# Window attention over a 511 x 511 image: one hand-ordered pipeline of blocks in place of a scheduled one

## The chip, the cores and the metric

The kernel runs on one core of a Trainium2 chip. The metric is the device time of one execution in microseconds (us). A core has a matrix engine (PE, with its weight loads in a row of their own, PEld), a vector engine (DVE), a scalar engine (ACT), GpSimd (POOL), and a sync engine (SP) that here only issues transfers. Sixteen DMA engines move data between the chip's memory (HBM) and the on-chip SBUF. PE writes to PSUM, from where DVE and ACT bring results to SBUF (an "eviction").

## The reference

```python
# x: 1 x 511 x 511 x 192, bf16; ws = 7, nh = 4 heads, dh = 48
pe = sum over the 3x3 taps of (x shifted) * dw_pe      # depthwise, zero padding
x0 = x + pe
h = layernorm(x0)                                      # over the 192 channels
hw = h cut into 73 x 73 windows of 7 x 7 = 49 tokens
q, k, v = split(hw @ w_qkv)
attn = softmax(einsum('whnm', q, k) * dh ** -0.5)
out = einsum('wnhd', attn, v) @ w_o
return x0 + out (windows put back)
```

There are 5329 windows of 49 tokens.

## The kernel before, in words

**Blocks.** 128 windows lie on the 128 partitions and make a block; 42 blocks cover the image in row order, the last with 81 windows. `XC` (two buffers) holds a block's pixels, 49 tokens x 192 channels in each partition; the convolution is added into it, and at the end the attention's output, and it is stored from there. `XP` (one buffer) holds the 9 x 9 patch around each window, transposed: patch position on 81 partitions, windows and channels along them.

**Convolution** (`conv_tile`, L274). For each channel one matmul of K = 81: the weights loaded are the patches `XP[0:81, :, c]` of 128 windows, every 192nd element of a partition, and the moving operand is a table `T` of 49 columns built once at the start. Twenty channels fill a PSUM buffer of two banks, and one DVE instruction (L284) adds them into `XC`.

**Layer norm.** `stats_part` (L301) gives DVE one `bn_stats` for each token, `stats_fin` a chain of small DVE instructions for 1/std. `build_D` (L324) lets POOL multiply the identity by 1/std, and `transposes` (L336) uses that diagonal as moving operand: seven matmuls bring seven tokens transposed and scaled into PSUM, and ACT or DVE (L355, L357) copies them to `hT`.

**Attention** runs over 16 groups of 8 windows in a block. `stage_A` (L402): q and k, 8 matmuls of 392 columns (L412) and their evictions (q in two halves into `Qb`, which is block-diagonal over pairs of heads, L421 and L422; k at L424 or L426), then v with 8 matmuls of 192 columns (L431, eviction L438). `stage_B` (L443): 16 matmuls of scores (L453) with all 128 rows and half of the array's columns each, and one exponential on ACT (L478). `stage_D` (L525): 32 matmuls (L532) on two 64 x 64 tiles of the array, a reciprocal and a multiplication on DVE (L543, L544). `stage_E` (L553): 8 matmuls against the identity turn the result (L560), and ACT copies it to `OT` (L567). `proj` (L359) multiplies `OT` by `w_o` when a block is done, with `XC` added by a matmul against the identity (L377) in one half of the buffers and by DVE (L378) in the other.

**What sets the order.** The main loop (L587) writes the stages down for group after group; a scheduler of the language may shift them within an engine. The convolution of the next block is written into groups 7 to 10 (`CONV0`, three `conv_tile` each), the statistics into groups 11 to 15, the transposes at a block's first group, `proj` and the store at group 3. All PSUM work goes through one ring of four two-bank buffers, `ps`. Loads of `XC` are on POOL's queue (L108); loads of `XP` (L139), in DMAs of nine patch rows by up to 73 windows with one 384-byte piece for each patch position and window, and the stores (L396) are on SP's queue.

Of the kernel before, what the change touches and what calls it, by code (L numbers as in the profile page):

```python
# [32 lines left out]
@with_exitstack  # L33
def _window_attn_kernel(ctx: ExitStack, tc: tile.TileContext, x, dw_pe, w_qkv, w_o, out, fast=None, eps=1e-5, logit_lim=40.0):
    nc = tc.nc
    _, H, W, C = x.shape
    WS, NH = 7, 4
    DH = C // NH
    S = WS * WS
    NWR, NWC = H // WS, W // WS  # L40
    NWIN = NWR * NWC
    BLK = 128
    NBLK = (NWIN + BLK - 1) // BLK
    KP = 81
    KT = C // 2
    CH = 8
    NCH = BLK // CH
    TOK = CH * S
    scale = float(DH) ** -0.5
    assert C == 192  # L50

    xr = x[0].rearrange("h (b q) c -> h b q c", q=WS)
    outr = out[0].rearrange("(a r) (b q) c -> a b r (q c)", r=WS, q=WS)
    xw = x[0].rearrange("(a r) (b q) c -> a b r (q c)", r=WS, q=WS)

    consts = ctx.enter_context(tc.tile_pool(name="consts", bufs=1))
    big = ctx.enter_context(tc.tile_pool(name="big", bufs=1))
    psum = ctx.enter_context(tc.tile_pool(name="psum", bufs=1, space=bass.MemoryType.PSUM))

    PS = _Rot([psum.tile([128, 1024], F32, name=f"ps{i}") for i in range(4)])  # L60
    for i, t in enumerate(PS.t):
        nc.vector.memset(t[:], 0.0)

    def two_bank(ps, ncol):
        return ps[:].rearrange("p (b n) -> p b n", b=2)[:, :, 0:ncol]

    ident = consts.tile([128, 128], BF, name="ident")
    make_identity(nc, ident[:])
    ones = consts.tile([128, 128], BF, name="ones")
    nc.vector.memset(ones[:], 1.0)  # L70

    XP = big.tile([128, BLK, C], BF, name="XP")
    XPf = XP[:].rearrange("p n c -> p (n c)")
    XC = [big.tile([128, S, C], BF, name=f"XC{i}") for i in range(2)]

    wq_sb = [consts.tile([128, 3 * C], BF, name=f"wq_sb{kt}") for kt in range(2)]
    Wo = [consts.tile([128, C], BF, name=f"Wo{kt}") for kt in range(2)]
    dwK = consts.tile([32, C], BF, name="dwK")
    nc.vector.memset(dwK[:], 0.0)
    for j in range(3):  # L80
        nc.sync.dma_start(out=dwK[9 * j : 9 * j + 3, :], in_=dw_pe[:, j, :])
    for kt in range(2):
        nc.scalar.dma_start(out=wq_sb[kt][0:KT, :], in_=w_qkv[kt * KT : (kt + 1) * KT, :])
        nc.scalar.dma_start(out=Wo[kt][0:KT, :], in_=w_o[kt * KT : (kt + 1) * KT, :])

    T = big.tile([128, C, S], BF, name="T")
    Sel = XC[1][:].rearrange("p n c -> p (n c)")[0:32, 0 : S * KP]
    nc.vector.memset(XP[:], 0.0)
    nc.vector.memset(XC[0][:], 0.0)

    def segments(blk):
        n0 = blk * BLK
        n1 = min(n0 + BLK, NWIN)
        segs = []
        n = n0
        while n < n1:
            a, b0 = divmod(n, NWC)
            b1 = min(NWC, b0 + (n1 - n))
            segs.append((a, b0, b1, n - n0))
            n += b1 - b0  # L100
        return segs

    def load_xc(blk):
        xc = XC[blk % 2]
        for (a, b0, b1, p0) in segments(blk):
            for o in range(0, b1 - b0, 16):
                nb = min(16, b1 - b0 - o)
                nc.gpsimd.dma_start(  # L108
                    out=xc[p0 + o : p0 + o + nb].rearrange("p (r q) c -> p r (q c)", q=WS), in_=xw[a, b0 + o : b0 + o + nb]
                )  # L110

    def load_xp(blk):
        for (a, b0, b1, p0) in segments(blk):
            nb = b1 - b0
            if a == NWR - 1 and blk > 0:
                nc.gpsimd.memset(XP[0:KP, p0 : p0 + nb, :], 0.0)
            else:
                if b0 == 0:
                    nc.gpsimd.memset(XP[0:9, p0 : p0 + 1, :], 0.0)
                if b1 == NWC:  # L120
                    nc.gpsimd.memset(XP[64:KP, p0 + nb - 1 : p0 + nb, :], 0.0)
            pr0 = 1 if a == 0 else 0
            pr1 = 8 if a == NWR - 1 else 9
            h0 = WS * a - 1
            for pc in range(9):
                if pc == 0:
                    q, sh = WS - 1, -1
                elif pc == 8:
                    q, sh = 0, 1
                else:  # L130
                    q, sh = pc - 1, 0
                bb0, bb1 = b0, b1
                if pc == 0 and bb0 == 0:
                    bb0 = 1
                if pc == 8 and bb1 == NWC:
                    bb1 = NWC - 1
                if bb1 <= bb0:
                    continue
                nc.sync.dma_start(  # L139
                    out=XP[9 * pc + pr0 : 9 * pc + pr1, p0 + bb0 - b0 : p0 + bb1 - b0, :],  # L140
                    in_=xr[h0 + pr0 : h0 + pr1, bb0 + sh : bb1 + sh, q, :],
                )


    load_xc(0)
    load_xp(0)

    nc.gpsimd.memset(Sel, 1.0)
    nc.gpsimd.affine_select(
        out=Sel,  # L150
        in_=Sel,
        compare_op=ALU.is_equal,
        fill=0.0,
        base=0,
        pattern=[[-1, WS], [-9, WS], [1, KP]],
        channel_multiplier=-1,
    )
    s0 = 0
    n = 0
    while s0 < S:  # L160
        ns = min(4, S - s0)
        ps = PS.next()
        for ss in range(ns):
            col = (ss // 2) * 512 + (ss % 2) * C
            nc.tensor.matmul(
                ps[0:KP, col : col + C],
                lhsT=Sel[0:21, (s0 + ss) * KP : (s0 + ss + 1) * KP],
                rhs=dwK[0:21, :],
                start=True,
                stop=True,  # L170
            )
        for bk in range((ns + 1) // 2):
            nn = min(2, ns - 2 * bk)
            dst = T[0:KP, :, s0 + 2 * bk : s0 + 2 * bk + nn].rearrange("p c s -> p s c")
            src = ps[0:KP, bk * 512 : bk * 512 + nn * C].rearrange("p (s c) -> p s c", c=C)
            if n % 2 == 0:
                nc.vector.tensor_copy(out=dst, in_=src)
            else:
                nc.scalar.copy(out=dst, in_=src)
            n += 1  # L180
        s0 += ns

    nc.vector.memset(XC[1][:], 0.0)

    Wqk = [consts.tile([128, 4, 128], BF, name=f"Wqk{kt}") for kt in range(2)]
    Wv = [consts.tile([128, C], BF, name=f"Wv{kt}") for kt in range(2)]
    pcs = PS.next()
    for kt in range(2):
        nc.tensor.matmul(pcs[:, 0 : 2 * C], lhsT=ones[0:KT, :], rhs=wq_sb[kt][0:KT, 0 : 2 * C], start=(kt == 0), stop=(kt == 1))
    for kt in range(2):  # L190
        nc.tensor.matmul(pcs[:, 512 : 512 + C], lhsT=ones[0:KT, :], rhs=wq_sb[kt][0:KT, 2 * C : 3 * C], start=(kt == 0), stop=(kt == 1))
    for kt in range(2):
        nc.vector.memset(Wqk[kt][:], 0.0)
        nc.vector.scalar_tensor_tensor(
            out=Wqk[kt][0:KT].rearrange("p m (h e) -> p (m h) e", e=64)[:, :, 0:DH],
            in0=pcs[0:KT, 0 : 2 * C].rearrange("p (g d) -> p g d", d=DH),
            scalar=-1.0 / C,
            in1=wq_sb[kt][0:KT, 0 : 2 * C].rearrange("p (g d) -> p g d", d=DH),
            op0=ALU.mult,
            op1=ALU.add,  # L200
        )
        nc.vector.scalar_tensor_tensor(
            out=Wv[kt][0:KT, :],
            in0=pcs[0:KT, 512 : 512 + C],
            scalar=-1.0 / C,
            in1=wq_sb[kt][0:KT, 2 * C : 3 * C],
            op0=ALU.mult,
            op1=ALU.add,
        )


    if fast is None:
        onesf = consts.tile([128, 1], F32, name="onesf")
        nc.vector.memset(onesf[:], 1.0)
        wsq = consts.tile([128, 2 * C], F32, name="wsq")
        nrm = [consts.tile([128, 8], F32, name=f"nrm{kt}") for kt in range(2)]
        for kt in range(2):
            nc.vector.tensor_tensor(out=wsq[0:KT, :], in0=wq_sb[kt][0:KT, 0 : 2 * C], in1=wq_sb[kt][0:KT, 0 : 2 * C], op=ALU.mult)
            nc.vector.tensor_reduce(out=nrm[kt][0:KT, :], in_=wsq[0:KT, :].rearrange("p (g d) -> p g d", d=DH), op=ALU.add, axis=AX.X)
# [14 lines left out]
    def main(fast):  # L234
      with ExitStack() as mctx:
# [342 lines left out]
        for it in range(NCT):  # L578
            conv_tile(0, it)
# [110 lines left out]
```

## Time and profile before

| what | us |
|---|---|
| median of three runs (5340.39 to 5368.98) | 5347.22 |
| span of the profiled execution | 5337.2 |
| PE busy, in all | 4490.1 |
| DVE busy | 3816.7 |
| ACT busy | 2744.5 |
| POOL busy | 758.0 |
| start, up to the first matmul of q | 157.5 |
| last block, from its first matmul of q | 94.6 |

The profiled span lies 10 us under the median. Between the start and the last block lie 41 blocks in 5085.1 us, 124 us each. In the profile a row of a group of instructions gives its line, engine, shape, count, busy time and the mean duration of one, and then what ended the engine's idle time before it. In a table of windows each row is a stretch of time with each engine's busy time in it, the granted PE clock (1.00 is full speed) and the DMA engines' busy share.

The rows of the matmuls give their latency (a matmul of 392 columns has 380 ns). In a stream they overlap, and what counts for PE is the distance from start to start: worked out from the trace's start times, the middle one is 170 ns in L412 (392 columns), 82 ns in L431 and L369 (192 columns), 55 ns in L346 (128 columns), 45 ns in L560 (98 columns) and 88 ns in L282, the convolution.

### The profile page before, as it was taken

The numbers are of one execution on the slowest core, as the hardware profiler recorded it, in microseconds if no ns is written. First come the engines' busy times: TensorE is split into PE (matmuls) and PEld (weight loads), VectorE is DVE, ScalarE is ACT, GpSimd is POOL, SyncE is SP. The second block draws the span as 40 slices with busy tenths as digits, with TensorE's granted clock in tenths as the row PEclk, the third lists the DMA queues.
The fourth block names the chain that finished last, engine by engine and source line by source line (L and its number), as shares of the span: only waits on it lengthen the run. The fifth ranks groups of instructions, "written<-read, shape, count | busy, mean of one in ns | idle before, by whom it ended". The sixth has DMA issues, their size and how long they took to land.

```text
span 5337.2 us, 148265 instructions
## 1 busy us (share of the span) xinstructions
PE 4490.1 (84%) x65427; PEld 3661.5 (69%) x65427; DVE 3816.7 (72%) x6912; ACT 2744.5 (51%) x3385; POOL 758.0 (14%) x833
## 2 busy tenths in 40 slices
PE   2788888888888888888988888888888888888887
PEld 1666676667776676677776777767666776677776
DVE  6776777767776777777677777777777777767776
ACT  1554555545555555555555455555555555545555
POOL 1111111111111111111111111111111111111120
PEclk9887888887778887888788877788888888877888
DMA  6554445554455555554455544455555445544431
GB/s 67 51 75 70 68 71 80 82 73 68 68 68 70 71 72 74 71 74 71 68 73 91 75 68 68 68 72 72 74 72 72 73 70 78 85 74 67 68 48 32
DMA packets 512613, 375.27 MB, mean 70 GB/s; under 512 B 453129, under 2 KB 453321, under 8 KB 511958
## 3 DMA queue, kind: packets, MB, share of 16 engines
q1 hardware_dynamic: 480918, 265.08, 38.1%
q0 software_dynamic: 30592, 100.32, 10.6%
q8 instruction: 514, 8.42, 0.7%
q14 instruction: 141, 1.16, 0.1%
q10 hardware_dynamic: 448, 0.30, 0.0%
HBM read 265.31 MB, written 100.27 MB: 68 GB/s over the span
## 4 chain that ended last, share of the span: by engine, by line
PE 44%; DVE 16%; ACT 14%; DMA 12%; SPq 9%; issue 4%; POOL 1%; DVEq 0%; ACTq 0%; POOLq 0%
PE ps L412 12%; PE ps L282 8%; SPq L396 7%; DMA out_dram<-XC 7%; PE ps L369 6%; DMA XC<-in_x_dram 5%; PE ps L453 5%; PE ps L532 4%; DVE kT L424 4%; ACT hT L355 4%; DVE Qb L422 3%; PE ps L431 2%; DVE XC L284 2%; PE ps L560 2%; ACT kT L426 2%
## 5 line engine op out<-in xcount | busy, mean ns | idle before, releaser
L412 PE MATMUL ps<-hT,Wqk 96*128 96x392 bf16 x5336 | 1233.5, 380 | 76.7 <-DVE XC L284 62.2
L478 ACT ACTIVATE PT<-ps 128x784 bf16<-128x784 f32 x667 | 552.7, 829 | 1095.3 <-PE ps L453 1080.3
L421 ACT CAST Qb<-ps 64x784 bf16<-64x784 f32 x667 | 555.3, 833 | 657.5 <-PE ps L412 655.7
L412 PEld LDWEIGHTS <-Wqk 96*128 96x128 bf16 x5336 | 529.4, 108 | 486.1 <-issue 252.5
L284 DVE TENSOR_TENSOR XC<-ps,XC 128x980 bf16<-128x980 f32 x378 | 437.9, 1176 | 503.0 <-PE ps L282 247.2
L282 PE MATMUL ps<-T,XP 81*128 81x49 bf16 x8064 | 744.0, 264 | 55.5 <-DMA XP<-in_x_dram 55.5
L567 ACT CAST OT<-ps 96x784 bf16<-96x784 f32 x667 | 541.0, 811 | 456.0 <-PE ps L560 452.4
L282 PEld LDWEIGHTS <-XP 81*128 81x128 bf16 x8064 | 733.9, 220 | 57.6 <-issue 55.5
L431 PE MATMUL ps<-Wv,hT 96*128 96x192 bf16 x5336 | 663.5, 277 | 16.4 <-DVE On L544 9.0
L532 PE MATMUL ps<-V,PT 49*64 49x49 bf16 x21344 | 542.5, 195 | 159.1 <-DVE Qb L422 81.2
L431 PEld LDWEIGHTS <-hT 96*128 96x128 bf16 x5336 | 548.8, 111 | 180.0 <-issue 91.6
L544 DVE TENSOR_TENSOR On<-ps,rs 128x768 bf16<-128x768 f32 x667 | 634.6, 951 | 16.0
L532 PEld LDWEIGHTS <-PT 49*64 49x64 bf16 x21344 | 466.2, 116 | 260.4 <-issue 217.7
L327 POOL TENSOR_TENSOR D<-ident,rstd 128x896 bf16<-128x896 bf16 x294 | 486.2, 1681 | 1074.8 <-DVE rstd L320 1053.3
L424 DVE CAST kT<-ps 128x784 bf16<-128x784 f32 x462 | 450.0, 974 | 219.2 <-PE ps L412 209.1
L304 DVE BATCH_NORM_STATS2 bnst<-XC 128x6 f32<-128x192 bf16 x2058 | 600.5, 343 | 0.2
L453 PE MATMUL ps<-Qb,kT 128*64 128x98 bf16 x10672 | 408.0, 225 | 180.7 <-DVE Qb L422 132.2
L422 DVE CAST Qb<-ps 64x784 bf16<-64x784 f32 x462 | 451.6, 978 | 110.6 <-ACT Qb L421 100.1
L355 ACT CAST hT<-ps 96x896 bf16<-96x896 f32 x462 | 452.4, 1109 | 135.9 <-PE ps L346 134.9
L560 PE MATMUL ps<-ident,On 128*96 128x98 bf16 x5336 | 412.1, 226 | 114.4 <-DVE kT L424 110.9
L453 PEld LDWEIGHTS <-kT 128*64 128x64 bf16 x10672 | 341.5, 121 | 231.5 <-issue 131.7
L108 POOL DMA_DIRECT2D XC<-in_x_dram x386 | 216.0, 560 | 1865.9 <-DVE rs L543 996.3
(73 smaller groups left out, 4396.2 us busy)
## 6 DMA issues: line engine op xcount, KB each, us to landing
XC<-in_x_dram POOLq DMA_DIRECT2D x277, 294.0 KB, 7.5
out_dram<-XC SPq DMA_DIRECT2D x277, 294.0 KB
XP<-in_x_dram SPq DMA_DIRECT2D x210, 246.4 KB
XP<-in_x_dram SPq DMA_DIRECT2D x68, 243.0 KB
XC<-in_x_dram POOLq DMA_DIRECT2D x37, 165.4 KB, 7.1
out_dram<-XC SPq DMA_DIRECT2D x37, 165.4 KB
XP<-in_x_dram SPq DMA_DIRECT2D x22, 216.0 KB
XP<-in_x_dram SPq DMA_DIRECT2D x18, 212.6 KB
```

The lines of the kernel that those rows point to most:

```text
L282: nc.tensor.matmul(ps[:, col : col + S], lhsT=XP[0:KP, :, c], rhs=T[0:KP, c, :], start=True, stop=True)
L304: nc.vector.bn_stats(out=bnst[:, s, :], in_=xc[:, s, :])
L355: nc.scalar.copy(out=hv[0:KT, kt, :, s0 : s0 + NDG], in_=src)
L412: nc.tensor.matmul(ps[:, ab * 512 : ab * 512 + TOK], lhsT=Wqk[kt][0:KT, which * 2 + ab, :], rhs=hT[0:KT, kt, ck * CH : (ck + 1) * CH, 0:S] ...
L421: nc.scalar.copy(out=dst[0:64, :, :, 0, :], in_=src[0:64])
L422: (nc.vector.tensor_copy if dve_help else nc.scalar.copy)(out=dst[64:128, :, :, 1, :], in_=src[64:128])
L424: nc.vector.tensor_copy(out=dst[:, :, 0:TOK], in_=two_bank(ps, TOK))
L431: nc.tensor.matmul(ps[:, col : col + C], lhsT=hT[0:KT, kt, ck * CH + 2 * jj : ck * CH + 2 * jj + 2, :].rearrange("p w s -> p (w s)"), rhs= ...
L453: nc.tensor.matmul(ps[64 * wp : 64 * wp + 64, col : col + 2 * S], lhsT=k_[:, ab, w * S : w * S + 64], rhs=q_[:, ab, w, :, :].rearrange("p ...
L478: nc.scalar.activation(out=pt[:, 0 : 16 * S].rearrange("p (b n) -> p b n", b=2), in_=two_bank(ps, 8 * S), func=ACTF.Exp, scale=scale,)
L532: nc.tensor.matmul(ps[64 * wp : 64 * wp + 64, col : col + S], lhsT=pt[64 * wp : 64 * wp + S, pc_ : pc_ + 64], rhs=v_[64 * wp : 64 * wp + S ...
L544: nc.vector.tensor_tensor(out=o_[:].rearrange("p (b j) (h d) -> p b (j h) d", b=2, d=DH), in0=ov[:, :, :, 0:DH], in1=r_[:].rearrange("p (b ...
```

## The change

The kernel is written anew, as a class, and the order within each engine is now fixed by hand (`tc.manual_schedule()`). What it computes is the same.

- **Blocks** are made of two strips of 64 windows (`_blocks`), 42 in all, the last with 81 windows. Pixels lie in `X`, three buffers. All loads and stores of full blocks are on SP's queue, in DMAs of 64 partitions: `X` row by row (14 DMAs for a block), stores in four chunks of rows (8 DMAs). `XP` keeps one buffer but is ordered by patch row first: a DMA's nine rows now go to partitions 9 apart, and not to nine neighbours.
- **Convolution**: same matmuls, in PSUM buffers of one bank (two of them, `psc`, shared with the transposes), ten channels each. They are put between the matmuls of q, k and v by `fill`, over the first 7.5 of a block's 16 slots; where a following block allows it, its first 30 channels are done in slots 14 and 15 already.
- **Layer norm**: `bn_stats` reads two tokens, interleaved, in one instruction (25 and not 49 for a block); POOL computes 1/std with a power and multiplies the pixels by it (`ln_norm`); PE transposes in its transpose mode with bf16 in PSUM (`ln_tr`); one half of each is copied by DVE, the other by ACT. This goes over slots 9 to 15, and the result goes to `HO`, two buffers, in which `stage_E` later puts the attention's output in the place of its own input.
- **Attention**: q is one eviction, no longer block-diagonal. Scores and attention times v are 32 matmuls each, in turn on all four 64 x 64 tiles. `stage_E` uses the transpose mode. All evictions of q, k and the exponential are on ACT; those of v on DVE in slots 0 to 7 and 15, on ACT otherwise; those of `stage_E` on DVE. The other PSUM ring has three two-bank buffers.
- **Projection**: two tiles of four tokens in each of slots 2 to 6, the rest in 7 and 8; ACT copies, POOL adds into `X`. The matmuls against the identity are gone.

```diff
-    XP[9 * pc + pr0 : 9 * pc + pr1, p0 + bb0 - b0 : p0 + bb1 - b0, :]
+    self.XPr = self.XP[0:KP].rearrange("(r q) n c -> q r n c", q=9)
+    dst = XPr[pc, pr0:pr1, p0 + n0 : p0 + n1, :]
...
-            for s in range(sa, sb):
-                nc.vector.bn_stats(out=bnst[:, s, :], in_=xc[:, s, :])
+            nc.vector.bn_stats(
+                out=bnst[:, s : s + 2, :].rearrange("p a f -> p (a f)"),
+                in_=self.X[b % 3][:, s : s + 2, :].rearrange("p s c -> p c s"),
+            )
+        def ln_norm(b, r, eng):
+            t = slice(r * WS, (r + 1) * WS)
+            e = nc.gpsimd
+            e.tensor_scalar(out=rstd[:, t], in0=bnst[:, t, 2], scalar1=1.0 / C, scalar2=self.eps, op0=ALU.mult, op1=ALU.add)
+            e.tensor_tensor(out=rstd[:, t], in0=rstd[:, t], in1=expo[:].to_broadcast([128, WS]), op=ALU.pow)
...
+            eng.tensor_tensor(
+                out=h[:, :, :], in0=self.X[b % 3][:, t, :], in1=rstd[:, t].unsqueeze(2).to_broadcast([128, WS, C]), op=ALU.mult
+            )
+        def stage_A(b, ck, which, fill):
...
+            for ab in range(2):
+                for kt in range(2):
+                    mm(
+                        ps[:, ab * 512 : ab * 512 + TOK],
+                        lhsT=self.Wqk[kt][0:KT, which * 2 + ab, :],
+                        rhs=HO[b % 2][0:KT, kt, ck * CH : (ck + 1) * CH, 0:S],
...
+                fill(2)
+            nc.scalar.copy(out=dst[:, :, 0:TOK], in_=two_bank(ps, TOK))
...
+                        for hp, cp in ((0, 0), (1, 1), (0, 1), (1, 0)):
+...
+                                tile_position=(64 * hp, 64 * cp),
...
+            conv_goal = base + part(0.0, 0.39 + d, C - base)
+            ahead = n and conv.c == C and early and xpn == len(xp) and xln == len(xl)
+            if ahead:
+                conv, conv_goal = nn.conv, 10 * part(0.875, 1.0, 3)
...
+            s_goal = part(0.40 + d, 0.87, len(n.items)) if n else 0
...
+                    goal = part(0.38 + d, 0.64 + d, len(xp), at)
+                    while xpn < goal:
+                        xp[xpn]()
...
+                stage_A(b, ck, 0, fill if not ahead else lambda w: None)
+                stage_E(*groups[g - LE], nc.vector.tensor_copy)
+                stage_A(b, ck, 1, fill)
+                stage_V(b, ck, fill, nc.vector.tensor_copy if idle else nc.scalar.copy, vv[g % 2])
...
+                stage_D(vv[(g - LD) % 2])
+                stage_B()
+                    n.transpose(part(0.50 + d, 0.96, WS), 1.0)
```

In a block in the middle, the matmuls of slots 0 to 6 hold 22 channels of convolution each and slot 7 holds 8; slots 2 to 6 have 16 matmuls of the projection, slot 7 has 8 and slot 8 has 10; slots 9 to 15 have 14 transposes of the layer norm each; slots 14 and 15 have 20 and 10 channels of the block after next. On SP's queue the 18 DMAs of `XP` begin behind the convolution's last matmul in slot 7; the stores of the last two chunks stand between them, and the 14 of `X` at their end and behind. DVE's first addition of channels in slot 14 waits for all DMAs of `X`.

## The prediction

> **What bounds the kernel now.** I read the page's busy times first, then a table of windows over one block, then the timeline of an ordinary slot, and last SP's queue.
>
> ```profile
> span 5337.2 us, 148265 instructions
> PE 4490.1 (84%) x65427; PEld 3661.5 (69%) x65427; DVE 3816.7 (72%) x6912; ACT 2744.5 (51%) x3385; POOL 758.0 (14%) x833
> ```
>
> No engine is full over the span, so the limit must change by stage. The table cuts the block that begins at 2018.4 us: two ordinary slots, the slot with the projection, four ordinary ones, the convolution, and slots with statistics and transposes.
>
> ```profile
> core 0: us, PE busy (x) PEld busy (x) DVE busy (x) ACT busy (x) POOL busy (x), PEclk, DMA share, GB/s
> 2018.36:2027.96 9.60, 7.72 (x148) 5.97 (x145) 7.94 (x9) 5.84 (x8) 0.00 (x0) 1.00 0.75 79
> 2027.96:2042.36 14.40, 13.97 (x197) 12.92 (x196) 10.42 (x13) 6.82 (x10) 0.00 (x0) 1.00 0.41 44
> 2042.36:2061.40 19.04, 15.40 (x293) 11.90 (x290) 15.88 (x19) 10.40 (x14) 3.48 (x7) 1.00 0.88 190
> 2061.40:2100.40 39.00, 36.24 (x414) 30.42 (x409) 23.36 (x26) 7.56 (x10) 1.55 (x3) 0.53 0.22 33
> ```
>
> The fourth row is the expensive one: 39 us in which ACT and POOL do nearly nothing and the PE clock is granted by half. In that stretch the trace has four groups' work and 192 channels in solid runs; a channel has 88 ns from start to start, of which its 49 columns fill a quarter, and the matmuls of q and k, 170 ns apart elsewhere, are 327 ns apart. Ordinary slots take 4.8 us, in which DVE has 4.1 us of work (0.26 + 0.95 + 0.97 + 0.98 + 0.96).
>
> ```profile
> 1903.04 0.54 PE L453 MATMUL ps<-Qb,kT 128*64 128x98 bf16 x16 [0.49 <-DVE Qb L422]
> 1903.51 0.69 PE L532 MATMUL ps<-V,PT 49*64 49x49 bf16 x32
> 1904.13 1.54 PE L412 MATMUL ps<-hT,Wqk 96*128 96x392 bf16 x8
> ```
>
> From start to start: scores 0.47 us, attention times v 0.62 us. SP's queue, columns start and length:
>
> ```profile
> 1854.07 54.74 SPq L139 DMA_DIRECT2D XP<-in_x_dram  x27
> ```
>
> One block's `XP`, 128 x 81 pieces of 384 bytes (3.98 MB), keeps the queue 54.7 us. Before, that lay beside slots 11 to 15 and the next block's first, and nobody waited.
>
> **PE, slot by slot.** q and k are unchanged, 8 x 170 = 1.36 us; v 8 x 82 = 0.66. `stage_E`: 128 columns and not 98, 8 x 55 (the distance in L346) = 0.44, before 0.36. Scores and attention times v, 32 matmuls each: the 0.62 us of 32 on two tiles is the upper end, half of it (four tiles fully beside each other) the lower; I take 0.5 each, nearer the row, since more pairs must also be issued. Together 3.46. A channel costs at most 88 ns; behind a matmul of 170 or 82 ns its weights load under that one, and the lower end is some 50 ns. I take 70: 22 channels 1.54. Projection, 16 x 82 = 1.31. So slots 0 and 1 are 5.0, slots 2 to 6 are 6.3, slot 7 is 4.7, slot 8 is 4.3.
>
> In slots 9 to 13 PE has 3.46 + 14 x 55 ns = 4.2, but DVE more: reciprocal and product 1.21, `stage_E`'s copy 0.9 (0.81 on ACT, 0.96 on DVE for such shapes), a transposed half 1.16 (L357), and 25 / 6.5 of the new `bn_stats`. Its row is 343 ns for 192 elements, 292 back to back (600.5 us for 2058); 192 elements more at about a nanosecond each make 0.49: 1.86. DVE: 5.1. The bounds are 0.3 (a faster read) and 0.69 (two old ones), 0.7 us a slot either way. Slots 14 and 15: 3.46 + 0.77 + 15 x 0.07 = 5.3 on PE.
>
> Sum: 10 + 31.5 + 4.7 + 4.3 + 25.5 + 10.6 = 86.6 us. An ordinary slot before stood 0.65 us over its fullest engine, one at ACT's limit (4.53 with 4.1 of work) 0.4; I add 0.4 a slot: 93 us for a block, where it is now 124 (5085 / 41).
>
> **What is moved beside this.** ACT per block: 48 evictions of q, k and exponentials at 0.83, seven v at 0.81, seven halves at 1.11, 13 copies at 0.8, together 64 us of 93; DVE about 77: both are hidden. POOL: 13 additions of 768 elements and 7 products of 1344 at 1.88 ns each (L327: 1681 ns for 896) are 18.7 + 17.6 us; DVE's instructions have no two SBUF inputs with them. Power of 128 x 7 has no row: 0.25 us (the small memsets, L119) is the floor; I take 1, and 5 as upper end. POOL then needs 7 x (2.5 + 0.25 + 1) = 26 us within slots 8 to 15, hidden; at 5 it is 54, some 12 more than is there. Adding the pixels on POOL removes 25 x 82 ns of identity matmuls and DVE's L378. The removed chain of small DVE instructions is in the 77.
>
> **The transfers.** This is where a new wait comes. `XP` has one buffer, so its load starts behind the convolution's last matmul in the middle of slot 7, 47 us into the block. Slot 14 needs it again, and DVE's first addition there needs all of `X`, at 84 us. All is on one SP queue: behind a late DMA wait the ones of `X`, behind DVE's addition everything DVE does for attention, and then PE. So 37 us must suffice for `XP`, two chunks of stores (384 pieces of 2688 bytes) and `X` (896). Such a piece takes 135 ns in the middle on SP's queue: (384 + 896) x 0.135 / 16 = 10.8 us.
>
> By the row `XP` takes 54.7 us again, a wait of 54.7 + 10.8 - 37 = 28 us. But its rows now lie nine partitions apart. [...] Counting the trace's 384-byte pieces by the microsecond gives 190 in the middle and 323 in the fastest hundredth, when DMAs have drifted apart. I take 323: 10368 / 323 = 32 us, 32 + 10.8 - 37 = 6 us of wait. A block: 99 us.
>
> **The clock.** [...] I take nothing, since q, k and v are in every slot.
>
> **Start, end, sum.** The start has 109.7 us until `XP` has landed, with DVE's zeroing ahead of it and two blocks' `XC` beside; alone with one block's `X` I estimate 32 + 18 + 10 for setting up = 60. Then channels 17 (192 x 88), statistics 12, seven rows of norm and transposes 25: 115, before 157.5. The last block: 11 slots at 4.9 and a final projection (8 us), store and two slots' rest: 80, before 94.6. 115 + 41 x 99 + 80 = 4254 us of span, and 10 more as for the median: 4264.
>
> **Rivals.**
> *No wait, four tiles at once.* `XP` at 26 us or less, scores at 0.31: nine PE-bound slots save 0.38 each, 90 us a block: 115 + 3690 + 80 + 10 = 3895. [...]
> *The load stays as it was.* 54.7 us, 28 of wait: 121 a block, 5170. For it: the row itself, the same nine rows by 64 pieces. Against: the new partitions.
> *Slower: the clock falls and stays down.* Before, a PE pause of 2.0 us at 2062.3 began the half-clock stretch, which held through all mixed slots until the channels were over. The new wait in slot 14 would start it, and channels follow until slot 7. At half clock the 69 us of a block's matmuls without channels become 138; ten of sixteen slots so add some 42 us: 141 a block, about 6000. It decides the sign from 39% of the block: 25 us up to 124, of 64 for all of it. Against: channels are now scattered in twos between matmuls of 392 columns, so no stretch is a quarter filled.
> *POOL is late.* Power at 5 us: 12 us more, about 111 a block, 4756.
>
> **Numbers.** Forecast (95 to 107 a block) 0.42; no wait 0.25; old rate 0.20; POOL 0.04; slower 0.09. The range 3870 to 5150 leaves out the slower case, the end of the old rate's and a tip below. More than 0.5% is about what a measurement here can tell: faster 0.90, within 0.01, slower 0.09.
>
> **What would show it.** Right: slots 2 to 6 near 6.7 us with PE over 90% busy and the clock at 1.00; SP's `XP` rows 30 to 35 us long; DVE's addition in slot 14 ended by a DMA, about 6 us. Wrong: `XP` at 50 us, or a clock under 0.9 in the windows of slots 0 to 8, or PE waiting for `h` from POOL. If the clock and the load are both as before, nothing of my sum holds but the start.

## The result, and the profile after

The changed kernel takes 4339.95 us (median of 4 runs, 4337.42 to 4344.01), the kernel before in the same session 5358.1 us (4 runs, 5340.39 to 5371.32): a ratio of 0.8105, interval 0.8083 to 0.8128. The forecast was 4264, so the direction and the order of size were right and 76 us are to be explained. Of one kernel below (e5) the executions lie at two levels, 4090 and 4152 to 4158 us, so that no interval is given for its ratio; its trace is one of the longer ones.

The page's head, beside the two lines that the prediction opens with:

```profile
span 4339.7 us, 166161 instructions
PE 3660.3 (84%) x75049; PEld 3194.9 (74%) x75049; DVE 2852.9 (66%) x4618; ACT 2519.7 (58%) x3128; POOL 2055.6 (47%) x1427
```

The PE's share is the same 84% although it has more matmuls: its busy time fell by 830 us. Its mean granted clock is 0.894 (before 0.824), and the quarter-filled runs of channels are gone; e3 below puts them back. DVE's busy time fell by 964 us, POOL's rose by 1298.

The second table of the prediction cut one block by stages. The same for the changed kernel, block beginning at 1618.98 us. The rows are slots 0 and 1, slots 3 to 5, slot 9, slot 10, slots 11 to 13, slot 14 and slot 15:

```profile
core 0: us, PE busy (x) PEld busy (x) DVE busy (x) ACT busy (x) POOL busy (x), PEclk, DMA share, GB/s
1618.98:1632.20 13.22, 12.47 (x221) 10.71 (x221) 6.78 (x11) 4.44 (x6) 0.00 (x0) 0.61 0.01 2
1638.50:1657.10 18.60, 17.77 (x379) 17.44 (x379) 12.57 (x20) 11.95 (x16) 9.79 (x7) 1.00 0.16 40
1673.20:1680.80 7.60, 5.02 (x109) 3.94 (x103) 4.29 (x8) 3.92 (x5) 7.36 (x7) 0.85 0.75 194
1680.80:1687.10 6.30, 6.30 (x106) 4.58 (x105) 4.00 (x8) 3.93 (x5) 5.21 (x5) 0.63 0.68 176
1687.10:1701.80 14.70, 12.85 (x309) 10.16 (x307) 12.79 (x23) 12.39 (x16) 11.52 (x10) 1.00 0.85 178
1701.80:1711.70 9.90, 6.01 (x125) 5.61 (x123) 5.82 (x11) 4.44 (x6) 6.49 (x4) 0.88 0.54 142
1711.70:1720.60 8.90, 6.67 (x116) 5.24 (x114) 5.68 (x8) 4.73 (x5) 0.00 (x0) 0.75 0.01 2
```

The row of 39 us at clock 0.53 is gone: mixed slots (row two) run at 6.2 us each with PE 96% busy at full clock. In its place stand three places with a low clock (0.61, 0.63, 0.75 to 0.88), and two rows, slots 9 and 14, in which PE has holes of 2.6 and 3.9 us. Counted over the blocks 2 to 38, half-clock stretches begin in slot 0 in 21 blocks of 37, in slot 9 in 28 and in slot 14 in 31; all of them together are 20.7 us of a block.

Each of the three places has its own releaser. In slot 9 (PE alone, then POOL alone) the first transposes of a block wait for POOL:

```profile
1676.27 0.44 PE L411 MATMUL ps<-q,k 48*64 48x49 bf16 x32
1679.30 1.73 PE L351 MATMUL psc<-ident,h 128*96 128x128 bf16 x14 [2.58 <-POOL h L341]
```
```profile
1672.85 2.14 POOL L483 TENSOR_TENSOR X<-X,pO 128x768 bf16<-128x768 bf16 x2 [3.19 <-ACT pO L479]
1674.95 0.21 POOL L338 TENSOR_SCALAR rstd<-bnst 128x7 f32<-128x7 f32 x1
1675.25 1.49 POOL L339 TENSOR_TENSOR rstd<-rstd,expo 128x7 f32<-128x7 f32 x1
1676.81 2.43 POOL L341 TENSOR_TENSOR h<-X,rstd 128x1344 bf16<-128x1344 bf16 x1
```

POOL comes from the last additions of the projection straight to the chain of three for the first row, 4.3 us with a power of 1.49. In slot 14 (block beginning at 1816.75) DVE's first addition waits for `X`, as foretold; the transposes behind it wait for a PSUM bank that this addition frees:

```profile
1906.61 0.56 DVE L457 COPY HO<-ps 96x784 bf16<-96x784 bf16 x1
1911.92 1.24 DVE L324 TENSOR_TENSOR X<-psc,X 128x490 bf16<-128x490 f32 x2 [4.75 <-DMA X<-in_x_dram]
1912.64 1.65 PE L351 MATMUL psc<-ident,h 128*96 128x128 bf16 x14 [2.37 <-DVE X L324]
```

At the turn of the block q waits for DVE's copy of the last transposed half. Over the whole span, by the waits of PE (columns: us in total, times, longest):

```profile
PE psc L351 <- DVE X L324: 98.4, 32, 4.1
PE psc L351 <- POOL h L341: 93.5, 38, 2.6
PE ps L373 <- DVE HO L361: 80.4, 42, 2.2
PE ps L432 <- DVE HO L457: 68.3, 130, 1.0
```

The first three rows are 272 us, and in most blocks half clock follows them (the counts above). SP's queue in the block that begins at 1816.75, `XP` from the convolution's end on and `X` behind it:

```profile
1868.29 1.70 SPq L239 DMA_DIRECT2D XP<-in_x_dram  x2
...
1883.12 8.46 SPq L239 DMA_DIRECT2D XP<-in_x_dram  x7
...
1899.58 8.86 SPq L255 DMA_DIRECT2D X<-in_x_dram  x11
```

In medians over blocks 2 to 38, counted from the start of the convolution's last channel in slot 7, the first 384-byte piece moves at 1.8 us and the last at 35.8, the last DMA of `X` leaves SP's queue at 39.8, its last piece has landed at 42.7, and DVE's addition starts at 43.4. This last number is the one to keep in mind.

### The profile page after: what moved, and what is told of

Its sections match the earlier page's. It is cut to its first block, busy times and chain, and to the rows that moved or that the text cites. A ratio compares the mean times of both kernels' runs of the same rounds, so it can differ in the third digit from the quotient of the medians.

```text
span 4339.7 us, 166161 instructions
## 1 busy us (share of the span) xinstructions
PE 3660.3 (84%) x75049; PEld 3194.9 (74%) x75049; DVE 2852.9 (66%) x4618; ACT 2519.7 (58%) x3128; POOL 2055.6 (47%) x1427
## 4 chain that ended last, share of the span: by engine, by line
PE 49%; DVE 21%; DMA 8%; ACT 8%; POOL 5%; SPq 5%; issue 4%; ACTq 0%; DVEq 0%; POOLq 0%
PE ps L373 18%; PE psc L318 8%; ACT pO L479 7%; PE ps L389 7%; PE ps L456 6%; DMA X<-in_x_dram 6%; PE ps L468 5%; DVE o L442 5%; DVE bnst L329 5%; DVE HO L361 4%; DVE v L397 3%; PE psc L351 3%; SPq L239 2%; DMA XP<-in_x_dram 2%; POOL h L341 2%
## 5 line engine op out<-in xcount | busy, mean ns | idle before, releaser
L483 POOL TENSOR_TENSOR X<-X,pO 128x768 bf16<-128x768 bf16 (+1 forms) x539 | 832.5, 1563 | 1934.2 <-ACT pO L479 1934.2
L373 PE MATMUL ps<-HO,Wqk 96*128 96x392 bf16 x5336 | 1473.2, 366 | 186.0 <-DVE HO L361 80.4
L318 PE MATMUL psc<-T,XP 81*128 81x49 bf16 x8064 | 1167.0, 216 | 86.9 <-DMA X<-in_x_dram 52.6
L381 ACT CAST k<-ps 128x784 bf16<-128x784 f32 x667 | 542.2, 813 | 521.6 <-PE ps L373 497.2
L419 ACT ACTIVATE pt<-ps 128x784 bf16<-128x784 f32 x667 | 550.5, 825 | 308.8 <-PE ps L411 292.9
L381 ACT CAST q<-ps 128x784 bf16<-128x784 f32 x667 | 542.7, 814 | 318.8 <-PE ps L373 271.9
L389 PE MATMUL ps<-Wv,HO 96*128 96x192 bf16 x5336 | 705.9, 257 | 25.6 <-ACT q L381 22.2
L341 POOL TENSOR_TENSOR h<-X,rstd 128x1344 bf16<-128x1344 bf16 x287 | 698.2, 2433 | 22.5
L442 DVE TENSOR_TENSOR o<-ps,rs 128x768 bf16<-128x768 f32 x667 | 638.5, 957 | 23.1
L389 PEld LDWEIGHTS <-HO 96*128 96x128 bf16 x5336 | 553.7, 111 | 105.7 <-issue 77.2
L456 PE MATMUL ps<-ident,o 128*96 128x128 bf16 x5336 | 473.1, 238 | 17.0 <-DVE o L442 14.3
L339 POOL TENSOR_TENSOR rstd<-rstd,expo 128x7 f32<-128x7 f32 x294 | 434.8, 1479 | 24.5
```

The lines of the kernel that those rows point to most:

```text
L318: mm(cv.ps[:, (c % 10) * S : (c % 10 + 1) * S], lhsT=XP[0:KP, :, c], rhs=T[0:KP, c, :], start=True, stop=True)
L341: eng.tensor_tensor(out=h[:, :, :], in0=self.X[b % 3][:, t, :], in1=rstd[:, t].unsqueeze(2).to_broadcast([128, WS, C]), op=ALU.mult)
L373: mm(ps[:, ab * 512 : ab * 512 + TOK], lhsT=self.Wqk[kt][0:KT, which * 2 + ab, :], rhs=HO[b % 2][0:KT, kt, ck * CH : (ck + 1) * CH, 0:S], ...
L381: nc.scalar.copy(out=dst[:, :, 0:TOK], in_=two_bank(ps, TOK))
L389: mm(ps[:, col : col + C], lhsT=HO[b % 2][0:KT, kt, w : w + 2, :].rearrange("p w s -> p (w s)"), rhs=self.Wv[kt][0:KT, :], start=(kt == 0) ...
L419: nc.scalar.activation(out=pt[:, 0 : 16 * S].rearrange("p (b n) -> p b n", b=2), in_=two_bank(ps, 8 * S), func=ACTF.Exp, scale=SCALE)
```

## The experiments

Eight more kernels ran, e1 to e4 on one chip and e5 to e8 on another, each beside the kernel before; kernels of different chips are compared by their ratios to it. The table has what their traces share: mean us of the slots, start of q to start of q, over blocks 2 to 39, and the median from the start of the last channel in slot 7 to DVE's first addition in slot 14.

| kernel | slots 0-3 | 4-8 | 9-13 | 14 | 15 | block | channel to addition |
|---|---|---|---|---|---|---|---|
| changed kernel | 26.3 | 28.8 | 27.7 | 9.9 | 8.5 | 101.2 | 43.4 |
| e1 rows on neighbours | 28.5 | 28.9 | 28.5 | 28.0 | 8.5 | 122.4 | 65.4 |
| e3 channels in solid runs | 34.0 | 43.0 | 27.2 | 10.2 | 8.2 | 122.5 | 43.8 |
| e4 two tiles at a time | 25.6 | 29.1 | 27.8 | 9.9 | 8.4 | 100.9 | 43.7 |
| e5 no channels ahead | 28.1 | 29.9 | 23.9 | 4.9 | 9.7 | 96.4 | none in 14 |
| e6 no power | 26.2 | 28.8 | 25.3 | 12.7 | 8.4 | 101.4 | 43.8 |
| e7 transposes a slot later | 27.8 | 28.8 | 23.5 | 14.3 | 11.0 | 105.4 | 44.0 |
| e8 idle matmuls | 23.6 | 28.8 | 26.2 | 11.7 | 8.8 | 99.2 | 43.6 |

**e1, the rows of XP on neighbouring partitions.** The one layout is undone in the changed kernel; the convolution's filter and the cleared rows follow it.

```diff
-        self.XPr = self.XP[0:KP].rearrange("(r q) n c -> q r n c", q=9)
+        self.XPr = self.XP[0:KP].rearrange("(q r) n c -> q r n c", r=9)
```

> The changed kernel with the nine rows of a patch DMA on nine neighbouring partitions again, as before the change; nothing else differs. [...] If the layout does not matter (the gain of the load comes from the order of the queue or from the absence of other transfers), 4340 us within 1%.

Measured: 5242.72 us (5233.33 to 5264.19), against 5332.13 before on that chip: 0.9835, interval 0.9798 to 0.9873. A block is 21 us longer, and all but 3 us of that is in slot 14. The wait of DVE there (DVE's waits of this kernel; its lines are one higher):

```profile
DVE X L325 <- DMA X<-in_x_dram: 935.0, 40, 32.9
```

In the changed kernel this row is 157.4 us over 33 times. The pieces now need 57 us from the first to the last instead of 34. Without this one line nearly the whole gain of the redesign is lost: with the old layout the same pipeline is worth 1.7% instead of 19%. The prediction's second rival (121 us a block) is what happens without the spread.

**e2, the spread alone in the kernel before.** The convolution's filter and the clearing of rows follow it here too.

```diff
-    XPf = XP[:].rearrange("p n c -> p (n c)")
+    XPr = XP[0:KP].rearrange("(r q) n c -> q r n c", q=9)
...
-                    out=XP[9 * pc + pr0 : 9 * pc + pr1, p0 + bb0 - b0 : p0 + bb1 - b0, :],
+                    out=XPr[pc, pr0:pr1, p0 + bb0 - b0 : p0 + bb1 - b0, :],
```

> The kernel before with one part of the change alone: the patch rows nine partitions apart. If the load was hidden there, as I hold, the XP load shrinks from 54 us to 35 or less and the time stays at 5340 to 5370 us. If transfers limited the kernel before, the time falls with the load, by up to 20 us a block, to about 4550 us.

Measured: 5284.23 us (5277.05 to 5302.57), 0.9909, interval 0.9873 to 0.9945. The load, from a block's first piece to its last, falls from 54 to 29.4 us in the median, but the blocks only from 124.0 to 123.3. One block's load on SP's queue, beside the row of 54.74 us in the prediction:

```profile
1820.04 31.93 SPq L139 DMA_DIRECT2D XP<-in_x_dram  x27
```

Its trace is 51 us shorter than that of the kernel before: 20.6 of it are the start and 30.5 all 41 blocks together. The load was hidden there, and making it shorter gains next to nothing; in the changed order the same edit is worth 21 us a block. The two parts of the change need each other.

**e3, the channels in solid runs.** `fill` is emptied, so that a slot's channels follow in one run behind v.

```diff
             def fill(weight):
-                quota[0] += (conv_goal - conv_start) * weight / (16 if ahead else 24)
-                while n and quota[0] >= 0.999 and conv.c < conv_goal:
-                    quota[0] -= 1.0
-                    conv_mm(conv)
+                return
```

> The changed kernel with the channels of a slot in one solid run behind v instead of scattered between the matmuls of q, k and v. If scattering hides weight loads and keeps the clock up, a channel goes from some 75 ns to 88 ns or more in seven and a half slots, and the solid runs of 2 us lower the clock in some of them: 3 us a block for the first alone (4460 us), up to 20 us a block with the clock (5160 us). If the gain comes from the cheaper evictions and the order between engines alone, the time stays at 4340 us within 1%.

Measured: 5214.35 us (5191.71 to 5232.17), 0.9771, interval 0.9728 to 0.9814. Slots 3 to 6 of one block by the windows:

```profile
core 0: us, PE busy (x) PEld busy (x) DVE busy (x) ACT busy (x) POOL busy (x), PEclk, DMA share, GB/s
2567.45:2606.82 39.37, 38.11 (x509) 31.40 (x505) 16.40 (x26) 16.19 (x20) 12.88 (x9) 0.67 0.15 37
```

9.8 us a slot at a clock of 0.67, where the same work with scattered channels takes 6.3 at 1.00 (6.2 in the second row of the block above). By the records the PE is 97% busy (38.11 of 39.37): a busy PE is not one at full clock. Half clock is 2409 us in all (926 in the changed kernel). So the prediction's case for "slower" had a real mechanism: with the channels in solid runs the clock goes down (0.67), with the same channels scattered it stays up (1.00), and without the scatter the gain over the kernel before falls to 2.3%. Even so a block is 122.5, not 141: the clock alternates, it does not stay down (271 of 308 half-clock stretches last 3.4 or 6.8 us).

**e4, attention's 32 matmuls two tiles at a time.** Only the order of the tiles changes, as in the kernel before.

```diff
-                    for row, cp, o in ((0, 0, 0), (1, 1, 1), (0, 1, 1), (1, 0, 0)):
+            for Q, h, tiles in [
+                (Q, h, t) for t in (((0, 0, 0), (1, 1, 1)), ((0, 1, 1), (1, 0, 0))) for Q in range(2) for h in range(NH)
+            ]:
```

> The changed kernel with scores and attention times v ordered so that only two of the four 64 x 64 tiles follow each other in turn, as before. If four tiles at once are what makes 32 matmuls take some 0.35 us and not 0.62, each slot gets 0.4 to 0.5 us more on PE; PE sets the pace in slots 0 to 8 and partly behind: 4 to 7 us a block, 4500 to 4630 us. If PE does not set the pace, 4340 us within 1%.

Measured: 4327.78 us (4314.36 to 4367.86), 0.8131, interval 0.8081 to 0.8182: the same as the changed kernel. The 32 do take longer, 0.41 instead of 0.26 us from the first start to the last. PE's timeline of an ordinary slot shows where that goes. Four tiles, in the changed kernel:

```profile
1858.04 0.44 PE L432 MATMUL ps<-v,pt 49*64 49x49 bf16 x32
1858.32 0.44 PE L411 MATMUL ps<-q,k 48*64 48x49 bf16 x32
1859.06 0.33 PE L373 MATMUL ps<-HO,Wqk 96*128 96x392 bf16 x1 [0.29 <-ACT pO L479]
```

Two tiles:

```profile
1822.28 0.50 PE L436 MATMUL ps<-v,pt 49*64 49x49 bf16 x26
...
1822.69 0.51 PE L413 MATMUL ps<-q,k 48*64 48x49 bf16 x27
1823.29 0.33 PE L373 MATMUL ps<-HO,Wqk 96*128 96x392 bf16 x1
```

With four tiles PE is done 0.29 us early and q waits for ACT's copy of the projection, which holds the PSUM buffer. With two tiles it is just in time. So slots 2 to 6 are not PE's: PE and ACT are level within 0.3 us.

**e5, no channels of the block after next in slots 14 and 15.** The kernel then begins each block with no channels done, and takes its later due times (d = 0.10 and not 0.07, half a slot) by itself.

```diff
-                early = nn and len(blocks[b + 2]) <= 2 and not any(ln[2] for ln in blocks[b + 2])
+                early = False
```

> The changed kernel without the convolution of the block after next in slots 14 and 15: all 192 channels of a block stay in slots 0 to 7. Theory A (the transfers limit slot 14: DVE's addition there waits 4.8 us for X): the wait goes, slots 14 and 15 fall from 18.3 to about 12 us, and the 30 channels that return to slots 0 to 7 cost 30 x 0.075 = 2.3 us less whatever of it hides, so about -4 us a block, 41 x -4 = -160 us: 4180 us. Theory B (the wait is the cover of something that is late anyway: SP's loads still end at 89 us of the block and the next block's slot 0 waits for HO): 4340 within 30 us or up to 100 us slower, with the time moved to slots 0 to 8.

Measured: 4154.62 us (4 runs, 4089.74 to 4157.77) against 5356.05 (7 runs, 5338.66 to 5367.2) before on that chip, 0.776 by the medians; its slowest run is below the fastest of the changed kernel. Slot 14 falls from 9.9 to 4.9 us, and DVE's wait there for `X` from 157.4 to 13.7 us. The last DMA of `X` leaves SP's queue 43.0 us behind the last channel, its last piece has landed at 45.8, and DVE's next addition comes at 48.2. So the wait goes, as Theory A said, and the total has the size it named (4.8 us a block, 4 on record), but the split is another: slots 14 and 15 take 3.7 us less and not 6, slots 9 to 13 take 3.9 less, and slots 0 to 8 take 2.8 more. What slots 9 to 13 gain fits the later due times that came along: e7 below, with later transposes and the channels ahead, gains 4.2 us there and loses it in slot 14. Later transposes do not pay by themselves, then, and probably do once nothing in slot 14 waits for the transfers; the two were not run apart. Left over is the half clock in slots 0 to 3, which take 28.1 us: PE still pauses for 2.28 us ahead of the last transposes in slot 15, and half clock begins in that slot in 36 of 37 blocks. Slots 0 to 3 of a short and slots 0 to 3 of a long block by the windows (columns as above; clock is the third from the end):

```profile
1731.38:1756.40 25.02, 23.66 (x482) 22.01 (x482) 15.47 (x25) 12.48 (x17) 3.96 (x3) 0.89 0.01 4
```
```profile
1252.60:1284.10 31.50, 31.15 (x482) 26.45 (x482) 15.83 (x25) 12.72 (x17) 3.90 (x3) 0.57 0.02 5
```

The same 482 matmuls, 25.0 or 31.5 us: after the same pause of 2.28 us the half clock lasted 6.8 us in one and 30.7 in the other. Most of its blocks are about 92 or about 99 us long, and this one difference is 6.5 us. It would explain the two levels of its time as well: the granted clock was 0.931 in the execution of 4090 us and 0.906 to 0.908 in the others, but only one of the longer ones has a trace.

**e6, no power on POOL.** A multiplication of the same operands stands in the place of the power, so that 1/std is left out.

```diff
-            e.tensor_tensor(out=rstd[:, t], in0=rstd[:, t], in1=expo[:].to_broadcast([128, WS]), op=ALU.pow)
+            e.tensor_tensor(out=rstd[:, t], in0=rstd[:, t], in1=expo[:].to_broadcast([128, WS]), op=ALU.mult)
```

> POOL's power is replaced by a multiplication of the same operands and tile, so that 1/std is left out and the output is not the reference's. Theory A (the 2.6 us pause of the PE at the first transposes of slot 9 comes from POOL's chain of 0.21 + 1.48 + 2.43 us, and brings 6 to 7 us of half clock with it): the power falls from 1.48 to about 0.2 us, the pause loses 1.3 us and the PE about 1 to 3 us of half clock after it: -2 to -4 us a block, 4340 - 41 x 3 = about 4220 us. Theory B (POOL is late because of the additions queued ahead of it, and slots 9 to 13 are set by DVE): no change within 30 us, slot 9 as before.

Measured: 4338.69 us (4312.06 to 4346.72), 0.8095, interval 0.8057 to 0.8134: nothing, and for neither theory's reason. The instruction fell from 1479 to 202 ns, PE's waits for `h` from 93.5 to 40.2 us, the blocks with half clock from slot 9 on from 28 to 6 of 37, and slots 9 to 13 by 2.4 us. Slot 14 grew by 2.8: DVE's wait there for `X` is 288.1 us instead of 157.4. Whoever comes to slot 14 sooner waits there longer, since the time from the last channel to this addition is what it was (43.8 us).

**e7, transposes a slot later.**

```diff
-                    n.transpose(part(0.50 + d, 0.96, WS), 1.0)
+                    n.transpose(part(0.57 + d, 0.96, WS), 1.0)
```

> The transposes of a row are asked for from 0.64 of the block instead of 0.57, one slot later. Theory A (the pause at the first transposes is a wait for POOL's h): the wait of 2.6 us and its half clock go (-3 to -5 us a block), but the last rows are bunched in slots 14 and 15, which may give back 1 to 3 us there: 4340 - 41 x 2 = about 4260 us. Theory B (the sum of the work on DVE and of the waits in slots 14 and 15 sets the block): the same within 40 us, the pause only moved. Slower than 4400 us if the last row then ends later and slot 0 of the next block waits longer than its 2.2 us.

Measured: 4502.65 us (4472.52 to 4520.35), 0.8401, interval 0.8355 to 0.8447: 3.7% slower than the changed kernel (0.8401 / 0.8105), the case that both theories had left for the end. The pause in slot 9 does go (slots 9 to 13 are 4.2 us shorter), slot 14 takes all of it back (+4.4), and the rows that are now bunched at the end cost 2.5 in slot 15 and 1.5 in slots 0 to 3 at a clock of 0.60 in slot 0.

**e8, idle matmuls in two of the pauses.** Nobody reads their result; they only keep the PE busy.

```diff
+        def warm(dst, count):
+            for _ in range(count):
+                mm(
+                    dst,
+                    lhsT=self.Wqk[0][0:KT, 0, :],
+                    rhs=self.Wqk[0][0:KT].rearrange("p m e -> p (m e)")[:, 0:TOK],
...
+                if kt == 0 and r == 0 and b > 0:
+                    warm(bank[:, 0:TOK], 12)
...
+            if which == 0 and ck == 0 and b > 0:
+                warm(ps[:, 0:TOK], 10)
```

> The changed kernel with 12 matmuls of 392 columns that nobody reads ahead of the first transposes in slot 9 and 10 ahead of the first q of a block, so that the PE is busy in two of its three pauses. Each takes 0.16 us at full clock: 12 are 2.0 us, 10 are 1.6 us, both about the length of the pause they fill. Theory A (half clock after a pause costs more than the pause): the half clock after those two falls from about 14 us a block to under 5, worth half of it where the PE sets the time: -3 to -6 us a block, about 4340 - 41 x 4.5 = 4155 us. Theory B (slots 0, 1 and 9 are not limited by the PE's clock, only by the waits themselves): 0 to +2 us a block, 4340 to 4420 us, though the half clock is gone.

Measured: 4274.98 us (4263.44 to 4289.12), 0.7991, interval 0.7961 to 0.8022, below the changed kernel's 0.8083 to 0.8128. Slots 0 to 3, slots 9 to 13 and slot 14 of one block by the windows, with idle matmuls first, the changed kernel behind it (columns as above):

```profile
1786.47:1809.16 22.69, 20.75 (x472) 20.36 (x472) 15.03 (x24) 12.02 (x16) 3.97 (x3) 1.00 0.01 3
1837.72:1863.53 25.81, 23.38 (x534) 17.84 (x523) 21.00 (x37) 20.20 (x25) 23.99 (x20) 1.00 0.78 186
1863.53:1875.91 12.38, 6.99 (x126) 6.42 (x124) 5.87 (x11) 4.42 (x6) 6.50 (x4) 0.67 0.67 147
```
```profile
1816.75:1846.67 29.92, 29.26 (x472) 25.32 (x472) 15.22 (x24) 12.15 (x16) 3.96 (x3) 0.60 0.01 2
1875.16:1903.41 28.25, 23.81 (x520) 18.46 (x511) 21.09 (x37) 20.26 (x25) 24.06 (x20) 0.88 0.72 175
1903.41:1914.09 10.68, 7.03 (x126) 6.47 (x125) 5.86 (x11) 4.43 (x6) 6.50 (x4) 0.68 0.63 161
```

The first rows hold the same 472 matmuls, 22.7 us at a clock of 1.00 and 29.9 at 0.60. With the two pauses filled, half clock begins in slot 9 in none of 37 blocks (before in 28) and in slot 0 in 3 (before in 21); in slot 14, which was left as it is, in 32. So it is the pauses that bring it. In the mean slots 0 to 3 gain 2.7 us; slots 9 to 13 gain 1.5, which slots 14 and 15 take back (1.9 and 0.3). The half clock falls from 926 to 551 us. Theory A holds for slots 0 to 3, which lie ahead of the last channel, and fails for slots 9 to 13, which lie behind it: 65 us and not 185.

**What they say together.** From the last channel to the addition in slot 14 it is 43.4 to 44.0 us in the changed kernel and the five others with its layout and channels in slot 14, whether slots 9 to 13 take 23.5 or 27.8 us; with the slow layout it is 65. So this part of a block is a chain of transfers, `XP`, two stores and `X`, and what PE, POOL and DVE do beside it is covered. Ahead of it and behind it PE's clock and the waits count in full. The gain of the redesign, 19%, is not a sum of parts: without the spread it falls to 1.7% (e1), without the scatter to 2.3% (e3). What the order by hand, the other evictions and the work moved to POOL are each worth was not run apart. Not tried either: e5 with idle matmuls ahead of its last transposes, and e5 with the earlier due times.

## Why the prediction was right, and where it was not

The direction and the size were right, the total 76 us short. By the prediction's own terms: 107.8 us until the first slot (115 on record), 41 blocks of 100.9 (99), 93.8 for the last block (80), together the span of 4339.7. Against 4264: -7 for the start, +79 for the blocks, +14 for the end, and -10 for the difference between span and median, which did not exist.

By slots, with the 0.4 of hand-over: slots 0 to 8 were put at 54.1 us and took 55.1; slots 9 to 13 at 27.5 and took 27.7; slots 14 and 15, wait included, at 17.4 and took 18.3. Within these sums errors cancel: slots 0 and 1 were put at 10.8 and took 12.7, slots 2 to 6 at 33.5 and took 32.4. That the sums agree so well is in part luck; the reasons one by one:

- **The transfers: right, in place and in size.** DVE's addition in slot 14 was to wait 6 us for `X`; it waits 4.8 (157.4 / 33). `XP` was put at 32 us and takes 34 from its first piece to its last. That is the forecast's mechanism. Its size was luck: it took the fastest hundredth of the old trace, 323 pieces in a microsecond, as the rate for all of them. That the new layout would bring this rate no row of the trace before shows, nor that the DMAs had drifted apart in that hundredth; the middle microsecond now holds 326, the fastest hundredth 474. e1 shows that it was the spread that did it (+21 us a block without it), and e2 that it was hidden before. The first two rivals are thereby both placed: the first (no wait) did not come, the second is e1.
- **"The clock ... I take nothing": this step failed.** The transposes alone do not let the clock down: slots 11 to 13, with 14 each, run at 1.00. What lets it down ahead of slot 0 and in slot 9 are pauses of up to 2.2 and 2.6 us: with them filled half clock begins there in 3 and in none of 37 blocks, before in 21 and 28 (e8; with slot 9's wait shortened, in 6: e6). The sum priced pauses only as waits, where it had them. Slots 0 to 3 without half clock are 2.7 us a block shorter (e8), more than the 1.9 that a block was off; of this, 65 us in all remained in the time of e8. The text even had the mechanism, in its case for "slower" (a pause of 2.0 us begins the half clock), and named a clock under 0.9 in slots 0 to 8 as a sign against itself; slots 0 to 2 have 0.77, 0.79 and 0.87 in the mean of the blocks. What it lacked was a middle value between no cost and 42 us.
- **POOL, "hidden": the reason failed, not the number.** PE waiting for `h` was one of the prediction's own signs of being wrong, and it came. The power is 1.48 us (1 on record), but the additions of the projection stand ahead of it, so the first `h` of a block is late by up to 2.6 us, 93.5 us in all. That POOL had room over slots 8 to 15 says nothing on when its first result comes. It costs nothing only because slot 14 waits anyway (e6).
- **PE's and DVE's slots.** Slots 2 to 6: 6.3 us and 0.4 of hand-over on record, 6.2 in the middle one (6.5 in the mean, with the half clock that reaches into slots 2 and 3); PE is busy 5.9 of that and then waits for ACT's copy (e4). In slots 4 to 6 q, k, v and `stage_E` take 3.60 us with their 22 channels, so a channel adds 52 ns (70 on record); 32 matmuls of attention take 0.28 us until the next ones start (0.5), and the 16 of the projection 1.6 (1.31). `stage_E`'s copy on DVE takes 0.57 us (0.9), a `bn_stats` 0.55 (0.49). By these DVE has 4.3 us in slots 11 to 13 and not 5.1; the excess was filled by the waits of slots 9 and 10, which were not foreseen. Two errors of opposite sign in one term.
- **The end.** The last block's final projections wait for ACT to copy them; 80 us had no such wait in it.

## What to carry to other kernels

Before a wait is priced, ask which stretch of the block it lies in: beside a chain of transfers of fixed length (here 43 us from the last reader of the buffer to the first user of the new data) a shorter wait, a faster engine or a higher clock are all worth nothing, and ahead of that chain each is worth its full length. A pause of PE of 2 us can cost more than itself when dense work follows: here, after a pause of 2.28 us, the clock came back only after 6.8 or 30.7 us in two blocks of e5; idle matmuls in two of the pauses were cheaper than the pauses (e8, 65 us), and work moved into them was not tried. And an early start of work (the 30 channels ahead) is only good if what it needs has come: here it set the engines to wait in order behind a transfer that nothing else needed yet.

## What was not expected of the hardware

- Half clock (0.50 in the records) comes in steps: of 91 stretches in 37 blocks of the changed kernel 33 last 3.4 us, 27 last 6.8, 16 last 10.2 and 15 last 13.7 to 23.9; with the slow layout (e1) up to 41. After the same pause it can be 6.8 or 30.7 us (e5), and nothing in these traces tells which it will be.
- Pauses of 2.2 to 2.6 us are followed by it, in most blocks: in the changed kernel half clock begins in slot 9 in 28 blocks of 37, behind a wait of up to 2.6 us, and in slot 0 in 21, behind one of up to 2.2. All these short pauses border on 14 transposes; whether the transposes have a part in it these runs do not tell.
- Nine partitions that lie nine apart took `XP` in the kernel before from 54 to 29.4 us (e2).
